# Second MLP: Strassen products accumulated on one another in open PSUM tiles instead of being added up in SBUF

## Chip, cores and metric

The kernel runs on one core of a Trainium2 chip. The metric is the device time of one execution in microseconds (us); of several executions the median counts.

## What is computed

Attention through packed keys, a squared-ReLU MLP, and a second MLP with a softmax and a layer norm between its two products. The change lies in the last function.

```python
def _moe_ref(x, w_in, w_out):                      # 4608 tokens, 512 -> 2048 -> 512
    h = np.maximum(x @ w_in, 0.0)
    return h * h @ w_out

def _moe2_ref(x, w_in, w_out, g_ln):               # 4608 tokens, 512 -> 1024 -> 512
    h = x @ w_in
    e = np.exp(h - np.max(h, axis=-1, keepdims=True))
    solu = h * (e / (np.sum(e, axis=-1, keepdims=True) + 1e-09))
    mu = np.mean(solu, axis=-1, keepdims=True)
    var = np.mean((solu - mu) ** 2, axis=-1, keepdims=True)
    return ((solu - mu) / np.sqrt(var + 1e-06) * g_ln) @ w_out
```

## The kernel before

Attention and the first MLP fill the execution up to about 800 us; their matmuls are those of line 58. The second MLP then goes over the 4608 tokens in 18 pairs of 128-token halves (256 tokens each). The loop at the end of `build` runs, for step `i`, `h2(i+1)` (first product, softmax, layer norm), `fetch_y` (loads the operands of a later pair), `ou(i-1)` (second product and output) and `tr(i)` (transposes of the normed rows and the operands of `ou`). `h2(0)` and the start of pair 1 lie inside the last steps of the first MLP.

Both products of a pair are done as 2 by 2 blocks by `strassen`, with seven block products instead of eight. `prod(l, r)` makes one block product: for each of `nk` chunks of 128 rows three matmuls (high part by high part, high by low, low by high, since every operand is split into two parts), all added up in one PSUM tile. In `h2` it has `nk` = 2 and 512 columns, so six matmuls a product, into tiles named `h`; in `ou` `nk` = 4 and 256 columns, twelve matmuls, into tiles `o`. The seven products are 11 by 11, 12 by 21, S2 by T2, S3 by T3, S1 by T1, S4 by 22 and 22 by T4; with the weights `wi0T2` (first chunk, operand T2) and `wx0` to `wx6` (11, T1, 22, 21, T3, T2, T4 of the first chunk) a row of TensorE tells which product it belongs to.

Before the change every product has a PSUM tile of its own. The first is copied out twice by ScalarE (lines 842 and 843). Three `add`s (`vadd`, line 854) bring products into the blocks `c12` and `c21` in SBUF on VectorE, and four `fin`s bring the rest; in `h2` `fin` is line 865, which also keeps the row maximum, in `ou` it is line 854 as well. So a row `hs L854` is an `add` of `h2`, a row `ys L854` an `add` or a `fin` of `ou`:

```python
        p1 = prod("11", "11")
        A.copy(c11, p1)
        A.copy(c12, p1)
        fin(0, c11, c11, prod("12", "21"))
        add(c12, c12, prod("S2", "T2"))
        add(c21, c12, prod("S3", "T3"))
        p5 = prod("S1", "T1")
        add(c12, c12, p5)
        fin(1, c22, c21, p5)
        fin(0, c12, c12, prod("S4", "22"))
        fin(1, c21, c21, prod("22", "T4"))
```

The tiles `h` and the tiles `o` have three PSUM banks each in the loop (`psh`, `pso`), with one more bank each for the transposes `ct`; pair 0 uses four banks that it shares with the first MLP. A product can begin when the product three before it in the same pool has been read.

In this part no order is written out. A scheduler sets it for each engine from its own estimates of durations, and an engine then does its instructions in that order: one that waits holds up all behind it on that engine. Other names: `ch`/`cl` are the high and low parts of `ou`'s operands (lines 1037 and 1038), `raw` the transposed blocks and their sums (lines 1053 and 1043), `e` the exponential (878), `hs` the rows of `h2` (`hs L891` and `hs L895` apply the layer norm), `rstd` a power on GpSimd (889).

## Time and profile before

| what | us |
|---|---|
| three executions | 1203.02, 1203.15, 1207.12 (median 1203.15) |
| profiled execution, first to last instruction (span) | 1198.6 |
| its TensorE busy | 1144.2 (95%) |
| its VectorE, ScalarE, GpSimd busy | 878.9, 665.0, 568.6 |
| TensorE's granted clock over the span | 0.990 |

The time of an execution is the span and some microseconds around it; the profiled execution's own time isn't among the three, so the difference between the median and the span, 4.55 us, is taken for what lies around. Instructions are counted busy from start to end. A matmul is pipelined: its end is modelled, and the next one starts before that end. So the spacing of the starts tells how fast TensorE works, and a row that TensorE "sat idle" before is a true wait.

### The profile page before, as it was taken

The page shows a single profiled execution, that of the slowest core. Times are in us where ns is not written, and L with a number is a line of the kernel's source. Part 1 is how long each engine was busy: PE and PEld are TensorE (multiplying, and loading weights), DVE is VectorE, ACT ScalarE, POOL GpSimd, SP SyncE. Part 2 cuts the span into 40 slices and gives each one's busy share as a digit, 9 for nine tenths or more (in the row PEclk, how much of TensorE's full clock was granted, in tenths as well). Part 3 has the DMA queues.
Part 4 walks back from the last instruction along what each step waited for, and adds up shares of the span by engine and source line. Part 5 has one row for each costly group of instructions (what it writes and reads, how often), then busy time and mean ns, then how long its engine had stood idle before and what let it go on. Part 6 is the DMA issues. An engine that isn't in the chain of part 4 may idle for free. (4 is left out here: it accounts for less than half of the span.)

```text
span 1198.6 us, 24126 instructions
## 1 busy us (share of the span) xinstructions
PE 1144.2 (95%) x8700; PEld 1049.8 (88%) x8700; DVE 878.9 (73%) x1705; ACT 665.0 (55%) x1510; POOL 568.6 (47%) x585
## 2 busy tenths in 40 slices
PE   6788999999999999999999999999999999999997
PEld 3466989898999998999998999988888899899897
DVE  4787688755326766567888977258989889889887
ACT  3575665344445555566675776435554655655554
POOL 0002354534225544475776775213754755745743
PEclk9889999999999999999999999999999999999999
DMA  9767697665155799779598796991133133223201
GB/s 326 229 185 204 181 300 234 211 210 197 57 200 151 207 302 298 215 276 334 203 384 316 257 379 245 387 342 74 61 133 102 41 132 106 84 84 111 80 23 49
DMA packets 124343, 236.99 MB, mean 198 GB/s; under 512 B 16576, under 2 KB 44224, under 8 KB 124224
## 3 DMA queue, kind: packets, MB, share of 16 engines
q1 hardware_dynamic: 124224, 235.46, 58.7%
q8 instruction: 68, 1.11, 0.4%
q14 instruction: 51, 0.42, 0.1%
HBM read 144.18 MB, written 91.23 MB: 196 GB/s over the span
## 5 line engine op out<-in xcount | busy, mean ns | idle before, releaser
L58 PE MATMUL Y<-ghl,woh 128*128 128x288 f32 x2048 | 463.9, 302 | 6.1 <-DVE yp L493 3.4
L58 PEld LDWEIGHTS Y<-ghl,woh 128*128 128x128 f32 x2048 | 345.4, 190 | 20.6 <-issue 6.1
L58 PE MATMUL Y<-ghl,wol 128*128 128x288 f32 x1024 | 304.2, 297 | 0.0
L58 PE MATMUL h<-ah,slot 128*128 128x288 f32 x1024 | 212.9, 296 | 10.3 <-ACT ah L432 9.0
L837 PE MATMUL o<-wx,ch 128*128 128x256 f32 x1008 | 190.2, 286 | 5.3 <-DVE ys L854 3.0
L58 PEld LDWEIGHTS Y<-ghl,wol 128*128 128x128 f32 x1024 | 194.6, 190 | 0.0
L1038 POOL TENSOR_TENSOR cl<-raw,ch 128x512 fp32r<-128x512 f32 x100 | 148.3, 1502 | 92.4 <-ACT ch L1037 47.0
L58 PEld LDWEIGHTS h<-ah,slot 128*128 128x128 f32 x1024 | 165.0, 189 | 12.6 <-ACT ah L432 9.5
L469 POOL TENSOR_TENSOR rg<-rg 128x288 f32<-128x288 f32 x128 | 92.8, 726 | 166.5 <-ACT rg L462 151.7
L837 PEld LDWEIGHTS o<-wx,ch 128*128 128x128 f32 x1008 | 158.9, 190 | 12.3 <-DVE ys L854 4.5
L58 PE MATMUL h<-al,slot 128*128 128x288 f32 x512 | 150.9, 295 | 1.0 <-DVE al L67 1.0
L837 PE MATMUL o<-wx,cl 128*128 128x256 f32 x504 | 142.1, 285 | 2.2 <-POOL cl L1038 1.7
L67 DVE TENSOR_TENSOR ghl<-rg,ghl 128x288 fp32r<-128x288 f32 x149 | 79.2, 537 | 80.2 <-POOL rg L469 63.2
L462 ACT ACTIVATE rg<-h 128x288 f32<-128x288 f32 x148 | 60.3, 408 | 98.0 <-PE h L58 95.0
L1037 ACT CAST ch<-raw 128x512 fp32r<-128x512 f32 x126 | 76.7, 622 | 61.0 <-DVE raw L1043 57.6
L53 DVE TENSOR_TENSOR ghl<-rg,ghl 128x288 fp32r<-128x288 f32 x107 | 78.2, 743 | 29.2 <-ACT ghl L53 15.6
L837 PEld LDWEIGHTS o<-wx,cl 128*128 128x128 f32 x504 | 95.4, 190 | 4.4 <-POOL cl L1038 2.5
L58 PEld LDWEIGHTS h<-al,slot 128*128 128x128 f32 x512 | 96.2, 188 | 1.6 <-DVE al L67 1.6
L53 ACT ACTIVATE rg<-h 128x288 f32<-128x288 f32 x108 | 44.3, 410 | 84.7 <-PE h L58 81.0
L837 PE MATMUL h<-wi,y 128*128 128x512 f32 x312 | 83.6, 402 | 0.3 <-DVE hs L854 0.3
L1043 DVE TENSOR_TENSOR raw<-raw 128x512 f32<-128x512 f32 x70 | 73.6, 1060 | 9.9 <-POOL cl L1038 5.0
L470 ACT ACTIVATE ghl<-rg 128x288 fp32r<-128x288 f32 x148 | 65.8, 445 | 20.6 <-PE Y L58 17.5
(172 smaller groups left out, 2097.7 us busy)
## 6 DMA issues: line engine op xcount, KB each, us to landing
pw_d<-pws SPq DMA_DIRECT2D x122, 256.0 KB, 4.5
slot<-pw_d SPq DMA_DIRECT2D x61, 512.0 KB, 6.0
yc_d<-yo SPq DMA_DIRECT2D x98, 256.0 KB, 5.6
y<-yc_d SPq DMA_DIRECT2D x92, 256.0 KB, 4.3
raw<-w_in SPq DMA_DIRECT2D x40, 512.0 KB, 6.5
raw<-w_out SPq DMA_DIRECT2D x24, 512.0 KB, 6.0
kf<-kT SPq DMA_DIRECT2D x32, 288.0 KB, 6.1
out<-ys SPq DMA_DIRECT2D x72, 128.0 KB, 1.7
```

Source lines behind the costliest of these rows:

```text
L53: return (lambda *a, **k: pin(fn(*a, **k))) if strict[0] else fn
L58: pin(PE.matmul(*a, **k))
L67: eng.tensor_tensor(out=lo, in0=x, in1=f(hi), op=ALU.subtract)
L462: A.activation(r, pb[:, :HF], AF.Relu)
L469: G.tensor_tensor(out=gg, in0=r, in1=r, op=ALU.mult)
L470: A.activation(gh, r, AF.Square)
L837: PE.matmul(bk, x, w[:, y], start=(i == 0), stop=(i == 3 * nk - 1))
L1037: A.copy(c[n][0], x)
L1038: eng.tensor_tensor(out=c[n][1], in0=x, in1=f(c[n][0]), op=ALU.subtract)
L1043: eng.tensor_tensor(out=out, in0=x, in1=y, op=op)
```

## The change

Products that share a sum are now accumulated on one another in one PSUM tile that stays open. `prod` takes a tile `bk` to go on with. Tile `u` takes 11 by 11, then S2 by T2, then S3 by T3; ScalarE copies it out after each of the three, into `c11`, `c12` and `c21`. Tile `p5` takes S1 by T1, is read by the `fin` of `c22`, and then takes S4 by 22. The three `add`s are gone and the four `fin`s stay; one copy by ScalarE is added, since there are three and not two. TensorE's matmuls are the same in number and kind. Between two products on one tile TensorE has to wait until the tile has been read; a Strassen now has four tiles and not seven.

```diff
-    def strassen(lhs, rhs, nk, N, pb, c11, c12, c21, c22, add, fin):
-        def prod(l, r):
-            bk = pb()[:, :N]
+    def strassen(lhs, rhs, nk, N, pb, c11, c12, c21, c22, fin):
+        def prod(l, r, bk=None):
+            new = bk is None
+            if new:
+                bk = pb()[:, :N]
             i = 0
             for k in range(nk):
                 lh, ll = lhs(l, k)
                 w = rhs[k][r]
                 for x, y in ((lh, 0), (lh, 1), (ll, 0)):
-                    PE.matmul(bk, x, w[:, y], start=(i == 0), stop=(i == 3 * nk - 1))
+                    PE.matmul(bk, x, w[:, y], start=(new and i == 0), stop=(i == 3 * nk - 1), skip_group_check=not new)
                     i += 1
             return bk
 
-        p1 = prod("11", "11")
-        A.copy(c11, p1)
-        A.copy(c12, p1)
+        u = prod("11", "11")
+        A.copy(c11, u)
         fin(0, c11, c11, prod("12", "21"))
-        add(c12, c12, prod("S2", "T2"))
-        add(c21, c12, prod("S3", "T3"))
+        prod("S2", "T2", u)
+        A.copy(c12, u)
         p5 = prod("S1", "T1")
-        add(c12, c12, p5)
+        prod("S3", "T3", u)
+        A.copy(c21, u)
         fin(1, c22, c21, p5)
-        fin(0, c12, c12, prod("S4", "22"))
         fin(1, c21, c21, prod("22", "T4"))
+        prod("S4", "22", p5)
+        fin(0, c12, c12, p5)
```

The two callers no longer hand `vadd` over. In the changed file the lines behind `strassen` stand three lower: 842/843 become 844, 847 and 850 (the copies of `u`), 854 becomes 857, 1037 becomes 1040.

The scheduler makes a new order of the second MLP. Three places show it. The first is the Strassen of pair 0 on TensorE, inside the first MLP; of the two chunks of a product the first stands here.

Before:

```order
L837 MATMUL h_10111<-wi011_9780,y0_9742 128x512 x3
...
L837 MATMUL h_10120<-wi021_9814,y0_9743 128x512 x3
...
L837 MATMUL h_10129<-wi0T2_9846,y0_9744 128x512 x3
...
L837 MATMUL h_10137<-wi0T3_9878,y0_9745 128x512 x3
...
L837 MATMUL h_10145<-wi0T1_9913,y0S1_9746 128x512 x3
...
L837 MATMUL h_10155<-wi022_9960,y0S4_9747 128x512 x3
...
L837 MATMUL h_10164<-wi0T4_9992,y022_9748 128x512 x3
...
L58 MATMUL Y0_618<-ghl_10015,woh9_2004 128x288
```

After, on the same engine at the same place:

```order
L839 MATMUL h_10111<-wi011_9780,y0_9742 128x512 x3
...
L839 MATMUL h_10119<-wi021_9814,y0_9743 128x512 x3
...
L839 MATMUL h_10135<-wi0T1_9913,y0S1_9746 128x512 x3
...
L839 MATMUL h_10111<-wi0T2_9846,y0_9744 128x512 x3
...
L839 MATMUL h_10111<-wi0T3_9878,y0_9745 128x512 x3
...
L839 MATMUL h_10135<-wi022_9960,y0S4_9747 128x512 x3
L839 MATMUL h_10135<-wi122_9962,y0S4_9747 128x512 x3
L58 MATMUL Y0_618<-ghl_10015,woh9_2004 128x288
...
L839 MATMUL h_10151<-wi0T4_9992,y022_9748 128x512 x3
```

S3 by T3 now comes directly behind S2 by T2 on the same tile `h_10111`, S4 by 22 directly behind S3 by T3, and 22 by T4 has gone behind twelve matmuls of the first MLP.

The second place is the Strassen of `ou` for pair 14, in the middle of the run, on TensorE; the first row of each product stands here. Before:

```order
L837 MATMUL o_14607<-wx0_9842,ch_14432 128x256 x2
...
L837 MATMUL o_14622<-wx3_9876,ch_14434 128x256 x2
...
L837 MATMUL o_14636<-wx5_9911,ch_14436 128x256 x2
...
L837 MATMUL o_14650<-wx4_9909,ch_14438 128x256 x2
...
L837 MATMUL o_14664<-wx1_9844,ch_14440 128x256 x2
...
L837 MATMUL o_14679<-wx2_9874,ch_14442 128x256 x2
...
L837 MATMUL o_14693<-wx6_9942,ch_14444 128x256 x2
```

After, for the same pair, with the product of `h2` (`h_14368`) and the transposes that stand between:

```order
L839 MATMUL o_14452<-wx0_9842,ch_14282 128x256 x2
...
L839 MATMUL o_14466<-wx3_9876,ch_14284 128x256 x2
...
L1036 MATMUL ct_14565<-ident_68,hs_14060 128x128 x3
L839 MATMUL o_14493<-wx1_9844,ch_14290 128x256 x2
...
L839 MATMUL o_14452<-wx5_9911,ch_14286 128x256 x2
...
L839 MATMUL h_14368<-wi022_9960,y2_14158 128x512 x3
...
L839 MATMUL o_14520<-wx6_9942,ch_14294 128x256 x2
...
L839 MATMUL o_14452<-wx4_9909,ch_14288 128x256 x2
...
L839 MATMUL o_14493<-wx2_9874,ch_14292 128x256 x2
```

Between two products on one tile the scheduler has put other products: 12 by 21 and S1 by T1 ahead of S2 by T2, 22 by T4 ahead of S3 by T3. On ScalarE the three copies of the same tile stand so, after the change:

```order
L1040 CAST ch_14292<-raw_14308 128x512
L850 COPY hs_14343<-h_14344 128x512
L844 COPY ys_14451<-o_14452 128x256
L847 COPY ys_14451<-o_14452 128x256
L1056 COPY raw_14570<-ct_14565 128x512
L881 ACTIVATE e_14403,sm3_14404<-hs_14342,nm2_14401 128x1024
L1040 CAST ch_14551<-raw_14570 128x512
...
L881 ACTIVATE e_14422,sm3_14423<-hs_14343,nm2_14420 128x1024
L850 COPY ys_14451<-o_14452 128x256
```

The first two copies follow each other, so ScalarE stands from the one to the end of S2 by T2; the third comes behind an exponential that waits for VectorE.

The third place is the last Strassen, that of `ou` for pair 17, at the end of TensorE's queue. Before:

```order
L837 MATMUL o_15200<-wx0_9842,ch_15141 128x256 x2
...
L837 MATMUL o_15229<-wx5_9911,ch_15145 128x256 x2
...
L837 MATMUL o_15257<-wx1_9844,ch_15149 128x256 x2
...
L837 MATMUL o_15243<-wx11_10022,ch_15147 128x256 x2
...
L837 MATMUL o_15272<-wx2_9874,ch_15151 128x256 x2
...
L837 MATMUL o_15286<-wx6_9942,ch_15153 128x256 x2
```

After:

```order
L1036 MATMUL ct_15000<-ident_68,hs_14612 128x128
L839 MATMUL o_15025<-wx0_9842,ch_14966 128x256 x2
...
L839 MATMUL o_14908<-wx2_9874,ch_14816 128x256 x2
...
L839 MATMUL o_15066<-wx1_9844,ch_14974 128x256 x2
...
L839 MATMUL o_15093<-wx6_9942,ch_14978 128x256 x2
...
L839 MATMUL o_15025<-wx4_9909,ch_14972 128x256 x2
...
L839 MATMUL o_15066<-wx2_9874,ch_14976 128x256 x2
```

The last product is now S4 by 22 on `o_15066`, directly behind S3 by T3; the `fin` that reads `o_15066` before it needs the copy of S3 by T3's tile.

## Rows read from the trace of the kernel before

**Rows 1.** The page's first line.

```profile
span 1198.6 us, 24126 instructions
```

**Rows 2.** Busy time by stretch: stretch, its length, PE, PEld, DVE, ACT, POOL, clock, DMA share, GB/s.

```profile
840.00:885.00 45.00, 41.69 (x278) 37.14 (x277) 43.36 (x88) 24.97 (x45) 30.62 (x26) 1.00 0.23 77
885.00:1160.00 275.00, 271.77 (x1763) 245.28 (x1762) 241.70 (x513) 156.75 (x279) 159.93 (x128) 1.00 0.28 91
1160.00:1198.60 38.60, 32.36 (x267) 31.46 (x265) 29.32 (x59) 17.10 (x31) 12.98 (x10) 1.00 0.13 42
```

**Rows 3.** PE's waits, 760 to 1199 us: us in total, times, longest.

```profile
PE o L837 <- DVE ys L854: 3.0, 3, 1.8
PE o L837 <- POOL cl L1038: 1.7, 2, 1.4
...
PE o L837 <- ACT ys L843: 1.2, 1, 1.2
```

**Rows 4.** Groups by line, 885 to 1160 us: count, busy us, mean ns, idle before.

```profile
L854 DVE TENSOR_TENSOR ys<-ys,o 128x256 f32<-128x256 f32 x85 | 33.7, 409 | 0.6 <-PE o L837 0.3
...
L854 DVE TENSOR_TENSOR hs<-hs,h 128x512 f32<-128x512 f32 x39 | 26.5, 679 | 1.5 <-PE h L837 0.5
...
L1038 DVE TENSOR_TENSOR cl<-raw,ch 128x512 fp32r<-128x512 f32 x12 | 10.8, 898 | 2.6 <-ACT ch L1037 2.6
...
L842 ACT COPY hs<-h 128x512 f32<-128x512 f32 x13 | 7.6, 586 | 0.0
...
L842 ACT COPY ys<-o 128x256 f32<-128x256 f32 x13 | 4.8, 368 | 0.0
```

**Rows 5.** Timeline (start, length, engine), one stop of PE and what ended it.

```profile
1140.78 0.40 PE L837 MATMUL o<-wx,ch 128*128 128x256 f32 x2
1141.02 0.28 PE L837 MATMUL o<-wx,cl 128*128 128x256 f32 x1
1141.89 0.50 PE L837 MATMUL o<-wx,ch 128*128 128x256 f32 x2 [0.60 <-DVE ys L854]
1142.24 0.28 PE L837 MATMUL o<-wx,cl 128*128 128x256 f32 x1
...
1141.42 0.42 DVE L854 TENSOR_TENSOR ys<-ys,o 128x256 f32<-128x256 f32 x1
```

**Rows 6.** Timeline of pair 0's Strassen: PE, then the first ACT copy and DVE `fin`.

```profile
778.70 2.98 PE L837 MATMUL h<-wi,y 128*128 128x512 f32 x12
781.52 0.86 PE L837 MATMUL h<-wi0T,y 128*128 128x512 f32 x3
...
787.51 0.93 PE L837 MATMUL h<-wi0T,y 128*128 128x512 f32 x3 [0.28 <-DMA wi0T<-wi_d]
788.68 0.96 PE L837 MATMUL h<-wi1T,y 128*128 128x512 f32 x3 [0.24 <-DMA wi1T<-wi_d]
...
780.31 0.58 ACT L842 COPY hs<-h 128x512 f32<-128x512 f32 x1 [0.46 <-PE h L837]
...
781.82 0.69 DVE L865 CUSTOM_DVE_ANT_0 hs<-hs,h 128x512 f32<-128x512 f32 x1 [1.21 <-PE h L837]
```

**Rows 7.** Timeline of the end: `h2`'s last matmuls, PE's last stops, DVE's last addition.

```profile
1159.38 0.86 PE L837 MATMUL h<-wi1T,y 128*128 128x512 f32 x3
...
1174.33 0.50 PE L837 MATMUL o<-wx,ch 128*128 128x256 f32 x2 [0.84 <-ACT ch L1037]
1176.39 1.07 PE L1033 MATMUL ct<-ident,hs 128*128 128x128 f32 x8 [1.55 <-DVE hs L891]
1177.98 0.39 PE L837 MATMUL o<-wx,cl 128*128 128x256 f32 x1 [0.52 <-DVE cl L1038]
...
1195.31 0.42 DVE L854 TENSOR_TENSOR ys<-ys,o 128x256 f32<-128x256 f32 x1 [1.01 <-PE o L837]
```

**Rows 8.** ACT's waits, 885 to 1160 us: us in total, times, longest.

```profile
ACT ch L1037 <- DVE raw L1043: 41.3, 30, 4.5
ACT hs L895 <- DVE nb L894: 17.8, 13, 2.9
```

## Prediction of the time after the change

> **What bounds the kernel now.** I read the busy time by stretch first. From 885 to 1160 us, thirteen of the eighteen pairs, TensorE is busy 271.77 of 275 us at the full granted clock, VectorE 241.70, ScalarE 156.75 [rows 2]. The change takes work from VectorE and leaves TensorE's matmuls as they are, so it can win only where TensorE stops; the second view is therefore TensorE's waits [rows 3]. VectorE's additions lead them with 3.0 us, and the 1.2 us for ScalarE's copy are theirs in part, since ScalarE's queue waits on VectorE too [rows 8]. All idle time of TensorE is 3.31 us from 840 to 885, 3.23 us from 885 to 1160, and 2.91 us in three stops near the end [rows 2, 7]. Pair 0 adds 0.28 and 0.24 us for weights [rows 6].
>
> A stop costs more than its idle row. In the timeline of one, two 256-column matmuls start 0.24 us apart, 0.12 each. The next ought to start at 1141.14 and starts at 1141.89; the one behind it comes 0.35 us later where 0.24 is usual [rows 5]. That is 0.75 + 0.11 = 0.86 us for a row of 0.60, so 0.26 us on top. With three, five and three stops the stretches hold 3.31 + 0.78 = 4.1, 3.23 + 1.3 = 4.5 and 2.91 + 0.78 = 3.7 us; pair 0 holds 0.52 + 0.52 = 1.0. Together 13.3 us, 1.1% of the time: no more is to be had.
>
> **The change, part by part.**
>
> *VectorE's additions.* Three of 679 ns and three of 409 ns go in every pair [rows 4], 3.26 us in some 21 us; at 88% busy [rows 2] that is about a sixth of its work. ScalarE gets one copy of 0.59 and one of 0.37 us more [rows 4], and was busy 57% of the stretch. Neither is worth anything in itself, since TensorE bounds both; worth lies in the stops. From 840 to 885, where VectorE is busy 43.36 of 45 us [rows 2], all three stops come from its lateness (1.8 us for an addition, 1.2 for a copy queued behind a cast that waited for it, and a small one). I take back three quarters: **-3.0** (bounds 0 and -4.1). From 885 to 1160 two stops for `ys` weigh 1.2 us idle (3.0 less the one of 1.8), two for GpSimd's `cl` 1.7 [rows 3], and the fifth, for an addition of `h2`, what is left of 3.23, 0.3. The additions' 1.5 us and 3 x 0.26 I take as gone, 2.3; `cl` is work that the change leaves alone, but in the new order S1 by T1, whose operand is ready earlier than S2's, is the third product, so of 1.7 + 0.52 I take half, 1.1: **-3.4** (bounds 0 and -4.5). What is late next is whatever else feeds TensorE: GpSimd's splits and ScalarE's casts.
>
> *The new waits in pair 0.* In the order, S3 by T3 follows S2 by T2 directly on one tile, and S4 by 22 follows S3 by T3 while `fin` still has to read its tile. Price of the first: the first product's six matmuls take 6 x 0.235 us (twelve take from 778.70 to 781.52), so it ends its turn at 780.11; the copy begins at 780.31 and takes 0.58 [rows 6]; TensorE resumes 0.05 us after a releaser ends [rows 5]. 0.20 + 0.58 + 0.05 + 0.11 of restart = 0.94 us. The second has a copy and a `fin` in a row: 0.20 + 0.58 + about 0.03 + 0.69 [rows 6] + 0.05 + 0.11 = 1.66. Nothing else stands on TensorE there, so nothing hides them: 2.6 us. ScalarE is free there and queues no more than the exponential behind the copies. Pair 1 has one product (1.4 us) between S3 by T3 and S4 by 22 where 1.55 are needed: 0.3. **+2.9** (bounds 2.5 and 4). On the other side 22 by T4 now comes after twelve matmuls of the first MLP, so its weights have landed: **-1.0**.
>
> *The new waits in the middle.* In pairs 2 to 16 I counted in the order what stands between two products on one tile. The shortest stretch in `ou` is 24 matmuls of 0.12 us, 2.9 us, and mostly 3.2 to 5; in `h2` it is 3.7. Needed are 0.20 + 0.37 + 0.05 = 0.62 and 0.83 us. So the copy hides, with at least 2.2 us to spare, as long as ScalarE comes to it in time. ScalarE does its queue in order, and ahead of the copies stand casts and exponentials that wait for VectorE; before, such casts waited 41.3 us in 30 waits, 1.4 each, 4.5 at the longest [rows 8]. Behind a copy that waits for TensorE stand the copies of `ct` to `raw`, on which VectorE and GpSimd wait; the order puts them where their transposes come later anyway. The trace of before has no such pair of products, so I bound it: 0 if every wait stays below 2.2, 7.7 if eight of sixteen pairs meet one of 2.9 (2.9 - 2.2 + 0.26 = 0.96 each). The mean of 1.4 is nearer to the lower end: **+1.5**.
>
> The Trainium skill speaks against this part: in "Perfetto Trace Analysis", section Matmuls, it asks that independent groups of matmuls rotate through PSUM banks, so that one is copied out while the next runs. By that rule each of the three stops of a chain would be paid in full; how much that is stands under the rivals. The order agrees with it in pair 0 and at the end, where the products do follow each other.
>
> *The end.* Before, the last matmul of `h2` ends at 1159.38 + 0.86 = 1160.24, and the last transposes start at 1176.39, after softmax and norm: 16.15 us [rows 7], with VectorE busy nearly all of it. In the new order VectorE has on that way four `ys` additions fewer and two `cl` splits more, -4 x 0.41 + 2 x 0.90 = +0.2 us [rows 4]; TensorE has 24 matmuls more and 7 transposes fewer to do meanwhile, some 2.0 us. So the two stops of 0.84 and 1.55 shrink to one of about 0.55. The last product is S4 by 22 behind S3 by T3: 0.20 + 0.37 + 0.03 + 0.42 + 0.05 + 0.11 = 1.2 us that nothing covers. With the stop of 0.52 for `cl`, 0.55 + 0.52 + 0.52 + 1.2 = 2.8 instead of 3.7: **-0.9** (bounds -2 and +1.5). Behind the last matmul stand, as before, one addition (1195.31) and the output's transfer.
>
> **Sum.** -3.0 - 3.4 + 2.9 - 1.0 + 1.5 - 0.9 = -3.9 us on the span of 1198.6 [rows 1]: 1194.7. The median of the runs, 1203.15, lies 4.55 us above the span, so 1199.3 us, 0.3% less. About 0.5%, 6 us, is what a measurement of this kernel can tell from no change.
>
> **The rivals.**
>
> *All old stops go and no new ones come in the middle.* -4.1 - 4.5 + 2.9 - 1.0 + 0 - 0.9 = -7.6, so 1195.6. For it: nearly all stops trace back to VectorE, which sheds a sixth of its work. Against it: GpSimd's two stops, and that the first pairs fill a pipeline in which something is late anyhow.
>
> *VectorE's relief buys nothing.* The scheduler's estimates stay what they were; if its order runs ScalarE's casts or GpSimd as late as VectorE ran, the old stops come back under other names. Then -1.0 + 2.9 = +1.9: 1205.1. For it: only 3.0 of TensorE's waits name an addition.
>
> *ScalarE comes late to the copies, slower than before.* A copy of `u` stands behind an exponential or cast that waits for VectorE, and TensorE stands behind the copy. If one wait of 2.9 us, as `hs` has it [rows 8], lies ahead of a copy in every one of sixteen pairs, it costs 16 x 0.96 = 15.4 us; with half of the relief (-3.2), +2.9, -1.0 and -0.9 that is +13.2, 1216.4. It ends above the old time from 2.2 / 16 = 0.14 us a pair, and above 0.5% from 0.5 us a pair. For it: the third copy of pair 14 stands behind an exponential. Against it: waits above 2.2 us were few, and a VectorE with a sixth less to do is late less often.
>
> *No overlap at all*, the skill's rule as a mechanism of this kernel: every copy stops TensorE. In `h2` 2 x 0.94 + 1.66, in `ou` 2 x 0.73 + 1.2, together 6.2 us a pair, 112 us in eighteen: 1315. The order has other products between in sixteen pairs, so this needs the order not to do what it says.
>
> **How the numbers follow.** Chances: the forecast 0.45 (1196.5 to 1203), all stops gone 0.22 (1194 to 1197), relief worth nothing 0.16 (1203 to 1207), ScalarE late 0.15, no overlap 0.02. The limits of 0.5% are 1197.1 and 1209.2. Faster: the second case and 0.05 of the first, 0.27. Slower: ScalarE late and no overlap, 0.17. The same: 0.56. The range from 1194 to 1207.5 holds the first three cases, 0.8 of the chance.
>
> **What would show it.** Right, if the stops for `ys` additions are gone from TensorE's waits, VectorE's share from 885 to 1160 falls to some 73%, TensorE waits about 0.8 us for a copy and 1.4 for a `fin` in pair 0, and about 1 us for a `fin` ahead of the last product. Wrong, if TensorE's waits name the copies (lines 844, 847, 850) in the middle, if its idle time there is not below 3.2 us, or if the last transposes wait for `hs` longer than before.

## The result, and the profile after

The changed kernel takes 1210.63 us (median of 6 executions, 1208.8 to 1212.01), the kernel before 1203.09 us (6, 1200.41 to 1207.12): 1.0057 times as long, 95% interval 1.0041 to 1.0073. That is slower by 0.6%, and above the predicted range (1194.0 to 1207.5). Executions of one kernel spread by some us with TensorE's granted clock: of 126 later ones of the kernel before, the 54 with a clock of 0.989 or more over the span have a median of 1201.8 us, the other 72 one of 1205.0; the changed kernel's six have clocks from 0.987 to 0.989.

The page's first line and the busy time by stretch (columns as in [rows 2], which these answer):

```profile
span 1208.4 us, 23964 instructions
```

```profile
840.00:885.00 45.00, 43.01 (x282) 38.74 (x282) 36.52 (x77) 29.58 (x57) 28.41 (x25) 1.00 0.24 77
885.00:1160.00 275.00, 269.65 (x1758) 243.53 (x1757) 216.25 (x443) 166.50 (x303) 147.75 (x127) 1.00 0.28 91
1160.00:1208.40 48.40, 41.13 (x303) 38.78 (x302) 32.30 (x60) 23.04 (x42) 17.32 (x13) 0.96 0.11 36
```

VectorE's busy time from 885 to 1160 us fell from 241.70 to 216.25 us (79% of the stretch, where 73% was predicted), and TensorE's fell as well, from 271.77 to 269.65: an engine with a tenth less to do, and TensorE stops more, not less (5.35 us idle, where the prediction called itself wrong from 3.2 on). TensorE's waits from 760 us on (us in total, times, longest), which answer [rows 3]:

```profile
PE o L839 <- DVE ys L857: 7.2, 6, 1.7
PE h L839 <- DVE mx L868: 2.1, 3, 1.4
PE ct L1036 <- ACT hs L898: 1.7, 2, 0.9
PE o L839 <- POOL cl L1041: 1.2, 1, 1.2
PE o L839 <- DVE cl L1041: 0.8, 1, 0.8
PE h L839 <- ACT hs L847: 0.7, 1, 0.7
PE h L839 <- ACT hs L850: 0.7, 1, 0.7
```

The additions' waits are gone, since there are no additions. In their place stand waits for `fin`s (`ys L857`, and `mx L868` in `h2`), and two of the transposes for the layer norm (`hs L898`).

To compare kernels I add up, over the whole timeline from the first `h2` matmul of pair 0 to TensorE's last matmul, by how much two successive matmuls start farther apart than the median of their kind. This holds the idle time, the slow start behind a stop, and lost clock. TensorE's work is the same in all kernels, so these sums must explain the difference, and they do: that distance is 416.29 us before and 423.48 after, 7.19 more, and the sums are 14.6 and 21.8.

| us lost by TensorE | pairs 0 and 1 (first 60 us) | 60 to 106 us (before: up to 885) | on to `h2`'s last matmul | the end | sum |
|---|---|---|---|---|---|
| before | 1.1 | 5.0 | 5.0 | 3.6 | 14.6 |
| changed | 4.3 | 2.7 | 7.8 | 7.1 | 21.8 |
| predicted change | +1.9 | -3.0 | -1.9 | -0.9 | -3.9 |
| measured change | +3.2 | -2.3 | +2.8 | +3.5 | +7.2 |

Ahead of pair 0 the program is the same, and executions differ by some us there by themselves (the first `h2` matmul starts at 778.70 in the profiled execution before, at 781.30 after).

**Pair 0.** TensorE's timeline (start, length) shows the two new waits:

```profile
787.74 0.97 PE L839 MATMUL h<-wi0T,y 128*128 128x512 f32 x3 [0.68 <-ACT hs L847]
...
790.82 1.43 PE L839 MATMUL h<-wi,y0S 128*128 128x512 f32 x5 [1.40 <-DVE mx L868]
```

With restarts they cost 0.83 and 1.57 us, where 0.94 and 1.66 were predicted; the waits for weights [rows 6] are gone, as predicted. **Pairs 1 and 2** were not foreseen so:

```profile
817.22 0.97 PE L839 MATMUL h<-wi,y 128*128 128x512 f32 x3 [0.68 <-ACT hs L850]
...
834.58 0.97 PE L839 MATMUL h<-wi,y 128*128 128x512 f32 x3 [0.50 <-DVE mx L868]
```

At 817.22 us TensorE waits for ScalarE's third copy. In the order the waiting product is 11 by 11 of pair 2, directly behind S3 by T3 of pair 1:

```order
L839 MATMUL h_10377<-wi0T3_9878,y1S3_9949 128x512 x3
...
L839 MATMUL h_10532<-wi011_9780,y2_10352 128x512 x3
```

It opens a new tile and needs a bank. Of the three, `p5` of pair 1 still holds one and 22 by T4 has another, so it takes that of `u`, which is free only when `u` has been copied out for the third time. I had priced the waits between two products on one tile, and not the next pair's wait for the bank that an open tile holds. With the restart it costs 0.83 us; the 0.3 us that I had ahead of S4 by 22 of pair 1 did not come, since this same product stands between. The stop at 834.58, 0.66 us with the restart, is of the kind that I had counted: S4 by 22 of pair 2 waits for the `fin` that reads its own tile. I had put that wait at nothing in pair 2; VectorE came to the `fin` only at 833.84, behind two `raw`.

**The middle.** It has four stops of over 1 us. Here is the first of them, PE's row first and then VectorE, ScalarE and GpSimd ahead of it:

```profile
922.45 0.50 PE L839 MATMUL o<-wx,ch 128*128 128x256 f32 x2 [1.66 <-DVE ys L857]
...
916.22 3.49 DVE L1046 TENSOR_TENSOR raw<-raw 128x512 f32<-128x512 f32 x2
919.63 1.25 DVE L897 SCALAR_TENSOR_TENSOR nb<-mv,rstd 128x1 f32<-128x1 f32 x1
920.80 1.27 DVE L887 BATCH_NORM_STATS2 st<-hs 128x6 f32<-128x512 f32 x2
922.00 0.39 DVE L857 TENSOR_TENSOR ys<-ys,o 128x256 f32<-128x256 f32 x1
...
918.09 0.62 ACT L1040 CAST ch<-raw 128x512 fp32r<-128x512 f32 x1 [2.11 <-DVE raw L1046]
...
915.49 6.60 POOL L1041 TENSOR_TENSOR cl<-raw,ch 128x512 fp32r<-128x512 f32 x4
```

The waiting product is S1 by T1 of a new pair. By the order it stands 4.9 us of TensorE's work behind S4 by 22 of the pair before, and of the three `o` banks the new `u` and the new 12 by 21 have two, so it needs the third, that of the old `p5`. VectorE had 4.9 us to read `p5`, but did two `raw`, a `nb` and two `st` first (`st` are the statistics for the norm), from 916.22 to 922.00: the `raw` took 1.74 us each and `nb`, the norm's bias, a column of 128x1, 1.25, beside GpSimd's `cl`. Five of the six waits for `ys` are of this kind, the first product on a new `p5` behind the late last `fin` of the old one; the sixth is the wait ahead of the last product (1.07 us; 1.2 predicted). Another such stop of 1.8 us comes at 1099.26, with the same instructions in the same order ahead of it, and two of 1.0 us for the layer norm at 967.12 and 1143.79.

**The end.** Two stops, with restarts 1.13 us for a `fin` and 1.38 for GpSimd's `cl`, and then the granted clock falls; behind it come two more, 0.95 us for a `cl` and the 1.07 ahead of the last product:

```profile
1180.66 0.50 PE L839 MATMUL o<-wx,ch 128*128 128x256 f32 x2 [0.97 <-DVE ys L857]
1182.39 0.39 PE L839 MATMUL o<-wx,cl 128*128 128x256 f32 x1 [1.23 <-POOL cl L1041]
...
1203.36 0.51 PE L839 MATMUL o<-wx,ch 128*128 128x256 f32 x2 [0.92 <-DVE ys L857]
```

Busy time by stretch:

```profile
1176.60:1182.60 6.00, 3.80 (x29) 3.40 (x29) 6.00 (x10) 2.64 (x6) 5.19 (x4) 1.00 0.20 67
1182.60:1186.60 4.00, 4.00 (x22) 4.00 (x22) 3.34 (x9) 1.67 (x3) 2.06 (x2) 0.57 0.12 39
```

From 1182.6 to 1186.6 us the granted clock is 0.57, mostly the lower level (1.2 of 2.4 GHz): 22 matmuls where a stretch as long in e6 (below) holds 36.

### The profile page after: what moved, and what is told of

The parts are those of the page before. It is cut to its first block, busy times and chain, and to the rows that moved or that the text cites. A ratio compares the mean times of both kernels' runs of the same rounds, so it can differ in the third digit from the quotient of the medians.

```text
span 1208.4 us, 23964 instructions
## 1 busy us (share of the span) xinstructions
PE 1146.8 (95%) x8700; PEld 1052.6 (87%) x8700; DVE 840.0 (70%) x1597; ACT 680.5 (56%) x1546; POOL 557.1 (46%) x585
```

## The experiments

Theories, as they came up: **A**, open tiles of `ou` hold its banks; **B**, it is the order that the scheduler made anew, and any edit moves the stops about; **C**, only the new waits of pair 0 and of the end count; **D**, the open tiles stretch `h2`, which then comes too late at the end; **F**, the end is limited by the last `ou` and VectorE; **G**, VectorE's relief went into waits for GpSimd; **H**, in `h2` it is `p5` that costs. For mixed kernels `strassen` has both forms:

```diff
+    def strassen(lhs, rhs, nk, N, pb, c11, c12, c21, c22, fin, add=None):
...
+        if add is not None:
+            p1 = prod("11", "11")
...
+            return
         u = prod("11", "11")
```

(between stands the form before the change, with seven tiles and three `add`s).

All results, with the lost time by stretch as in the table above (sums are of the profiled execution, medians and intervals of all):

| run | us, median | ratio to before, 95% interval | pairs 0, 1 | to 106 us | middle | end | sum |
|---|---|---|---|---|---|---|---|
| e1 `h2` alone | 1214.67 | 1.0079 to 1.0123 | 5.7 | 2.1 | 9.2 | 10.5 | 27.4 |
| e2 `ou` alone | 1196.22 | 0.9924 to 0.9956 | 1.1 | 2.8 | 3.0 | 3.9 | 10.7 |
| e3 `u` alone | 1204.39 | 0.9994 to 1.0021 | 4.0 | 4.1 | 2.5 | 5.6 | 16.2 |
| e4 `p5` alone | 1207.97 | 1.0026 to 1.0055 | 1.8 | 3.2 | 10.8 | 3.5 | 19.2 |
| e5 last `h2` old | 1212.69 | 1.0046 to 1.0096 | 4.3 | 2.7 | 7.6 | 10.6 | 25.1 |
| e6 pair 0 old | 1206.26 | 1.0000 to 1.0035 | 2.8 | 2.4 | 7.8 | 5.6 | 18.6 |
| e7 `ou` but the last | 1199.28 | 0.9951 to 0.9986 | 1.1 | 2.7 | 2.1 | 5.6 | 11.5 |
| e8 order of lines alone | 1204.13 | 0.9988 to 1.0027 | 2.7 | 5.0 | 6.7 | 3.4 | 17.8 |
| e9 short `nb` | 1203.63 | 0.9970 to 1.0009 | 4.2 | 2.3 | 3.1 | 6.6 | 16.1 |
| e10 `ou`, and `u` of `h2` | 1206.14 | 1.0004 to 1.0036 | 4.4 | 5.0 | 3.2 | 5.6 | 18.3 |
| e11 `ou`, short `nb` | 1198.00 | 0.9931 to 0.9973 | 2.0 | 0.8 | 4.5 | 2.7 | 10.0 |
| e12 `ou`, and `p5` of `h2` | 1202.79 | 0.9967 to 1.0004 | 2.2 | 3.5 | 4.6 | 5.5 | 15.9 |
| e13 long `nb`, order of e9 | 1204.82 | 0.9992 to 1.0024 | 4.2 | 2.5 | 4.2 | 6.6 | 17.5 |
| e14 short `nb`, order of e9 | 1204.25 | 0.9985 to 1.0019 | 4.1 | 2.0 | 2.7 | 5.9 | 14.7 |
| e15 before, short `nb` | 1197.23 | 0.9916 to 0.9966 | 1.2 | 1.6 | 3.5 | 4.0 | 10.3 |
| e16 pairs 0, 1 old, short `nb` | 1196.77 | 0.9929 to 0.9967 | 1.6 | 0.1 | 2.8 | 6.5 | 11.0 |
| e17 another order | 1201.78 | 0.9959 to 1.0002 | 4.8 | 1.6 | 1.0 | 6.0 | 13.3 |
| e18 `h2` alone, short `nb` | 1212.81 | 1.0051 to 1.0108 | 7.2 | 1.6 | 5.7 | 10.9 | 25.4 |

### Which half, which tile (e1 to e4)

```diff
-                 ob[0][0], ob[0][1], ob[1][0], ob[1][1], fin)
+                 ob[0][0], ob[0][1], ob[1][0], ob[1][1], fin, vadd)
```

This is e1; e2 has the same edit in `h2`'s call instead.

> The open tiles in h2 alone (products of 512 columns, pair 0 among them); ou adds up in SBUF as before. Reference points: 1203.1 us before, 1210.6 after. Theory A (open tiles of ou hold two of its three banks, so that a product stands until a late addition of VectorE has freed its bank): the loss lies in ou, so this keeps only pair 0's 1.6 us net and gains from 39 hs additions gone; about 1202 to 1205, and no stop above 1.2 us for a ys addition behind 885 us beyond the two of before. Theory B (the scheduler's new order as such: any change of the code moves some stops about): anywhere from 1200 to 1210, and the changes of the two halves do not add up to 7.5 us. Theory C (VectorE's relief is worth nothing, and only the new waits of pair 0 and of the end count): 1203.1 + 1.6 = 1204.7, the stretch from 885 to 1160 us as before (3.2 us idle).

> The open tiles in ou alone (products of 256 columns); h2 adds up in SBUF as before, also in pair 0. Theory A (banks of ou held by open tiles): the ys waits of TensorE, 7.2 us in six stops in the changed kernel, come back here, against 3.0 in three before; 1207 to 1210. Theory B (order as such): anywhere from 1200 to 1210. Theory C (only pair 0 and the end): 1203.1 plus the end's 3.9 us, 1207.0, with 3.2 us idle from 885 to 1160 us.

It came out the other way round. With open tiles in `ou` alone the kernel is 7.7 us faster than before, with open tiles in `h2` alone 10.7 us slower. Theory A, as a loss that lies in `ou`, fell. TensorE's waits of e2 (its `strassen` stands lower, so 857 is 830 here), and of e1:

```profile
PE o L842 <- DVE ys L830: 3.0, 4, 0.9
PE ct L1050 <- ACT raw L1070: 1.0, 1, 1.0
```

```profile
PE o L842 <- ACT ch L1054: 8.3, 6, 2.9
PE h L842 <- DVE mx L882: 3.7, 3, 1.9
PE o L842 <- DVE cl L1055: 2.4, 1, 2.4
```

In e1 TensorE waits for `ou`'s operands (`ch`, `cl`), which are made from `h2`'s result through norm and transposes.

For e3 and e4 one of the chains is taken apart, in both halves, first `p5` (e3), then `u` (e4):

```diff
         p5 = prod("S1", "T1")
+        vadd(c12, c12, p5)
...
-        prod("S4", "22", p5)
-        fin(0, c12, c12, p5)
+        fin(0, c12, c12, prod("S4", "22"))
```

```diff
-        u = prod("11", "11")
-        A.copy(c11, u)
+        p1 = prod("11", "11")
+        A.copy(c11, p1)
+        A.copy(c12, p1)
...
-        prod("S2", "T2", u)
-        A.copy(c12, u)
+        vadd(c12, c12, prod("S2", "T2"))
...
-        prod("S3", "T3", u)
-        A.copy(c21, u)
+        vadd(c21, c12, prod("S3", "T3"))
```

> In both halves only tile u stays open (11 by 11, S2 by T2, S3 by T3); S4 by 22 has a tile of its own, and one addition on VectorE (c12 plus S1 by T1) is back, so five tiles in a Strassen and one bank held throughout instead of two. Theory A: a fin of p5 no longer holds a bank until the end of the Strassen, so of the 7.5 us about half is gone: 1205 to 1208, with ys waits of TensorE around 3 to 5 us. Pair 0 keeps its copy's wait of 0.9 us but not the 1.6 us before S4 by 22. The end has no wait for a fin ahead of the last product (1.1 us less). Theory B: anywhere from 1200 to 1210. Theory C: pair 0 and the end are worth 2.7 us less than in the changed kernel, 1207.9.

> In both halves only tile p5 stays open (S1 by T1, then S4 by 22); 11 by 11, S2 by T2 and S3 by T3 have tiles of their own and two additions on VectorE are back, so six tiles in a Strassen. Theory A: one bank held from S1 by T1 to the last fin; the loss of 7.5 us falls by about half: 1205 to 1208. Theory B: anywhere from 1200 to 1210. Theory C: of the new waits pair 0 has one (a fin only, 0.2 + 0.7 + 0.2 = 1.1 us less the product ahead of it), the end keeps its 1.1 us: 1206 to 1208. If VectorE's load counts, this and the kernel with u alone lie between the two: VectorE's share from 885 to 1160 us about 84% here, 81% there, 79% with all chains and 88% before.

E4 lies between before and changed; e3 can't be told from before. In e4 the middle loses 10.8 us, nearly all of it in one kind of wait, S4 by 22 of `h2` for the `fin` that still reads its tile (eight of these nine waits; the first is pair 0's):

```profile
PE h L842 <- DVE mx L867: 9.0, 9, 1.5
```

That is the wait that the change adds, paid, with 0.3 to 1.7 us a time, where the scheduler puts S4 by 22 too early. In e3 the middle loses 2.5. Set against before, the medians of the two halves add up to +3.0 us and those of the two chains to +4.4, where the change costs 7.5. Either the parts work on one another or the new order of each kernel does it; these runs don't separate the two.

### The end and pair 0 (e5, e6), the last Strassen (e7), the order of lines (e8)

```diff
-                 t[0][:, 0], t[0][:, 1], t[1][:, 0], t[1][:, 1], fin)
+                 t[0][:, 0], t[0][:, 1], t[1][:, 0], t[1][:, 1], fin, vadd if m >= NPAIR - 1 else None)
```

This is e5; e6 has `m == 0` as the condition.

> The changed kernel, but h2 of the last pair (17) adds up in SBUF as before. In the order nothing moves ahead of that pair, and behind the last matmul of h2 there are 31.2 us of TensorE's work instead of 27.9 (31.3 before). In all six kernels measured so far 33.8 to 36.5 us pass from the last h2 matmul to the last matmul of all, whatever work is left for it (25.8 to 31.6 us). Theory D (the open tiles stretch h2's Strassen; the last h2 comes out later, and the chain softmax, norm, transposes, products behind it stays as long with less work to cover it): about 3.3 us less than the changed kernel, and 1 to 2 more if the granted clock no longer falls near 1181 us; 1205 to 1207.5. Theory B (any change of the order moves the stops about): no reason for a gain here; 1210.6 within 2 us. Theory F (the end is limited by the last ou's own chain and by VectorE, not by when the last h2 comes): 1210 to 1212, with the last h2 earlier and the same end.

> The changed kernel, but h2 of pair 0 adds up in SBUF as before; the order behind pair 1 is that of the changed kernel. The stops of 0.83 and 1.57 us for the copy and the fin of pair 0 go, the waits for the weights of T2 or T4 come back (0.52 idle, 1.0 with restarts): 2.4 + 0.2 - 1.0, so 1.2 to 1.6 us less than the changed kernel, 1209.2. If the time goes into the waits behind it instead (pair 1's 0.83 and 0.66, VectorE's and ScalarE's queues behind the first pairs), 1210.6.

In e5 the stops ahead of the last pair come back to a hundredth (1.82 us at the same place, 1.03, 0.34, 1.82, 1.04): the same order gives the same stops in another execution. The last `h2` did come earlier, 384.80 us behind the first instead of 388.26, and the end took 42.0 us instead of 35.2, with new stops of 3.2, 1.7 and 1.5 us and a fall of the clock. So Theory D's constant end fell: what is behind the last `h2` depends on the order as well. F came near in the time, but its end that stays the same did not show either: this one is 6.8 us longer, and the kernel is not faster.

E6 gains 4.4 us in the medians, more than the 1.2 to 1.6 expected, and 3.2 us in the sums: 1.5 in pairs 0 and 1, as expected, and 1.5 at the end, because the clock did not fall in the profiled execution. Its end has the same stops (1.15 and 1.38 us for 1.13 and 1.38), and the stretches that answer to those of the changed kernel read

```profile
1175.20:1181.20 6.00, 3.79 (x29) 3.38 (x29) 6.00 (x8) 2.41 (x4) 5.74 (x4) 1.00 0.15 49
1181.20:1185.20 4.00, 4.00 (x36) 4.00 (x35) 2.25 (x6) 2.17 (x5) 0.55 (x1) 1.00 0.07 19
```

E7 is e2 with the last Strassen of `ou` as before:

```diff
-                 ob[0][0], ob[0][1], ob[1][0], ob[1][1], fin)
+                 ob[0][0], ob[0][1], ob[1][0], ob[1][1], fin, vadd if m >= NPAIR - 1 else None)
```

> Open tiles in ou of pairs 0 to 16 only; h2 everywhere and ou of the last pair as before the change. Differs from the kernel with open tiles in all of ou (1196.2) in the last Strassen alone, where the last product waited 0.95 us for a fin. Theory D: that wait goes and the rest stays, 1.0 us less: 1195.2. Theory B: anything from 1194 to 1204. If the addition that is back on VectorE at the very end stands in the output's way instead, 1196 to 1197.

The wait of 1.08 us ahead of the last product is gone; one for `cl` grew from 0.95 to 2.43 us in its place, and the end is no shorter (5.6 us instead of 3.9): the 1.0 us less that Theory D had did not come. E8 is the kernel before with two of its lines moved:

```diff
-        add(c21, c12, prod("S3", "T3"))
         p5 = prod("S1", "T1")
+        add(c21, c12, prod("S3", "T3"))
         add(c12, c12, p5)
         fin(1, c22, c21, p5)
-        fin(0, c12, c12, prod("S4", "22"))
         fin(1, c21, c21, prod("22", "T4"))
+        fin(0, c12, c12, prod("S4", "22"))
```

> The kernel before with the products written in the new order (S1 by T1 third, 22 by T4 sixth, S4 by 22 last), but each in a tile of its own and with the three additions: nothing is accumulated across products. Matmuls, copies and additions are those of before, so only the scheduler's order differs. Theory B (order luck): it may lie as far from 1203.9 as the other kernels do, 5 us or more to either side. Theory D: h2 of the last pair spans 15.2 us of TensorE's work (12.9 before, 19.2 in the changed kernel) and 30.5 us are left behind it instead of 31.3: 0.8 us more at the end, so 1204 to 1206.

No difference in time that the runs can tell, though the stops lie elsewhere. Theory B allowed 5 us or more to either side; this order did not move the time.

### VectorE and GpSimd (e9 to e14)

In the changed kernel VectorE shed 35 of the 85 `ys` additions of [rows 4] and all 39 of `hs` from 885 to 1160 us, 35 x 0.409 + 39 x 0.679 = 40.8 us, and its busy time fell by only 25.4. Three groups that answer to [rows 4]:

```profile
L1046 DVE TENSOR_TENSOR raw<-raw 128x512 f32<-128x512 f32 x49 | 52.5, 1084 | 2.7 <-POOL cl L1041 2.4 <-ACT raw L1056 0.3
...
L1041 DVE TENSOR_TENSOR cl<-raw,ch 128x512 fp32r<-128x512 f32 x13 | 16.8, 1291 | 4.0 <-ACT ch L1040 3.9
L897 DVE SCALAR_TENSOR_TENSOR nb<-mv,rstd 128x1 f32<-128x1 f32 x19 | 16.0, 841 | 2.7 <-POOL rstd L892 2.7
```

`cl` has 1291 ns instead of 898, `nb` 841 instead of 321 (6.1 us in 19 before). These two grew by 6.0 and 9.9 us, 15.9 in all; `raw`, the costliest, did not grow (56.5 us in 52 before). Set against GpSimd's rows, the 15 `nb` that overlap one take 1023 ns, the other four 156; `raw` 1119 and 684, `cl` 1472 and 684. A `fin`, which reads PSUM, takes 0.4 us either way. The Trainium skill, "SBUF — State Buffer", section "Who interferes with whom", says that an instruction of VectorE with two inputs from SBUF contends with one of GpSimd that reads SBUF, and one with at most one such input doesn't, outside VectorE's two-port modes; the rows of `nb`, `raw`, `cl` and `fin` agree. The condition matters here: the norm's `hs L894`, with one such input of 128x1024, takes 812 ns alone and 1774 beside GpSimd's `cl`, so it is not so that all instructions with one input take the same, as the expectation below has it. So `nb` in a form with one input:

```diff
-                V.scalar_tensor_tensor(out=nb, in0=mv[:, 0:1], scalar=-1.0, in1=rstd, op0=ALU.mult, op1=ALU.mult)
+                V.tensor_scalar(out=nb, in0=rstd, scalar1=mv[:, 0:1], scalar2=-1.0, op0=ALU.mult, op1=ALU.mult)
```

> The changed kernel with one small instruction of VectorE in another form: nb (the norm's bias, 128x1) by a tensor_scalar with one input from SBUF and the mean as its scalar, instead of a scalar_tensor_tensor with two inputs from SBUF. In the changed kernel nb took 156 ns where GpSimd was idle and 1023 ns in the 15 of 19 times where GpSimd was running, as the subtractions of two SBUF inputs do (684 and 1119 ns), while VectorE's instructions that read PSUM or one input take the same with and without. Theory G (VectorE's relief was lost to waits for GpSimd, and its late fins and late nb make the four stops of 1.82, 1.82, 1.04 and 1.04 us in the middle): nb at about 150 ns throughout, each of the four stops shorter by about 1.1 us or gone, all stops from the first h2 matmul on 18 us instead of 22; 1206 to 1207.5. Theory B (the order as such): nb shorter as well, but the stops as large in other places, 20 to 24 us in all; 1209 to 1212.

7 us less than the changed kernel, below both forecasts, and the middle lost 3.1 instead of 7.8: it looked like Theory G. But the edit changes the scheduler's estimate too, and the order with it. Beside it other mixtures were run: e2 with one chain of `h2` added (e10 the `u` of e3, e12 the `p5` of e4, in the branch `if add is not None` that `h2` takes), and e2 with the short `nb` (e11).

```diff
+        if add is not None:
+            u = prod("11", "11")
...
+            fin(0, c12, c12, prod("S4", "22"))
+            return
```

> Open tiles u and p5 in ou, and in h2 tile u alone (its S4 by 22 in a tile of its own, one addition back). Between the kernel with open tiles in ou alone (1196.2, stops of 10.9 us from the first h2 matmul on) and the changed kernel (22.1 us). Theory H (in h2 it is tile p5 that costs: S4 by 22 waits for a fin that stands late in VectorE's queue, as the 9.0 us of mx waits with p5 alone): here only pair 0 and pair 1 pay 0.83 us each for a copy and the middle stays near 2 to 3 us; 1198 to 1200. Theory D (each chain stretches h2, 17.7 us of TensorE's work against 14.6): 27.9 us are left behind the last h2 matmul instead of 31.6, and the middle pays as well; 1201 to 1205.

> Open tiles in ou alone, with nb in the form of one input. In the kernel with open tiles in ou alone nb met GpSimd only 2 times in 18, so Theory G gives little: 0 to 1.5 us less than that kernel, 1195 to 1196.5. Theory B: the order moves once more, 1194 to 1202.

> Open tiles u and p5 in ou, and in h2 tile p5 alone (11 by 11, S2 by T2 and S3 by T3 in tiles of their own, two additions back). Theory H (tile p5 of h2 is what costs): pair 0 pays 1.6 us, and mx waits come back in the middle, 5 to 9 us in all; 1203 to 1207. Theory D (any chain in h2 stretches it): 30.0 us are left behind the last h2 matmul, 1.6 less than with ou alone; 1199 to 1203.

H fell: added to `ou`, tile `u` of `h2` costs 9.9 us and `p5` 6.6 (1206.14 and 1202.79 less 1196.22), more than the predicted 2 to 4 for `u`, and `u` more than `p5`. E11 is within 2 us of e2, on the slower side.

To tell G from B, `nb` got a form with two inputs that the scheduler prices as e9's, so that all engines have e9's order:

```diff
+                V.scalar_tensor_tensor(out=nb, in0=rstd, scalar=mv[:, 0:1], in1=mone, op0=ALU.mult, op1=ALU.mult)
```

This is e13; e14 has e9's line, and the constant `mone` of -1 as well, which it doesn't use.

> The changed kernel in the order of the kernel with nb of one input, on every engine, but nb again as a scalar_tensor_tensor with two inputs from SBUF (rstd and a constant -1, the mean as scalar). Theory G (two inputs from SBUF make nb wait for GpSimd, and that makes the stops): nb at 0.9 to 1.0 us wherever GpSimd runs (14 of 20 times), and stops in the middle of 5 to 8 us instead of 3.0; 3 to 5 us more than e14. Theory B (the order is what helped): nb long as well, but the stops as in e14 to 1 us.

> The partner of e13: the changed kernel with nb of one input (206 ns), with the same order. Under both theories the stops of the kernel measured before in this form: 3.9 us in pairs 0 and 1, 2.1 up to 885 us, 3.0 in the middle, 4.5 at the end (and 2 more where the granted clock falls); 1203.6 within 2 us.

```profile
L899 DVE SCALAR_TENSOR_TENSOR nb<-rstd,mv,mone 128x1 f32<-128x1 f32 x20 | 17.1, 854 | 2.4 <-POOL rstd L894 2.3
```

```profile
L899 DVE TENSOR_SCALAR nb<-rstd,mv 128x1 f32<-128x1 f32 x19 | 3.9, 207 | 2.8 <-POOL rstd L894 2.7
```

In one order `nb` takes 13.2 us more in e13 than in e14, and VectorE is busy 7.0 us more from 885 to 1160 us (216.23 and 209.18). That is worth 1.5 us in the middle, less than Theory G had (2 to 5) and more than Theory B (1). Of the 2.8 us in all sums 1.7 are a fall of the clock at 1177 us that only e13's profiled execution has; the medians lie 0.6 us apart, which the runs can't tell from nothing. So of e9's 4.7 us in the middle some 1.5 were `nb` at most, and the rest the order. Only `nb` was tested so: what the two `raw` beside `cl` cost (1.74 us each at the first stop, 0.68 alone) has no such pair of runs.

### The order itself (e15 to e18)

E15 is the kernel before with e9's line for `nb`.

> The kernel before the change with nb of one input. There nb met GpSimd 6 times in 19, 0.53 us each, 3.2 us of VectorE's time in the middle, and no stop of TensorE named the norm. Theory G: 0 to 1.5 us less than before, 1202 to 1204. Theory B: the order moves, 1199 to 1208. If nb's form is worth as much here as in the changed kernel (7 us), it has nothing to do with the change: 1196 to 1197.

The kernel before gains 6 us by the same edit of `nb`, close to the third forecast, though only 6 of its 19 `nb` met GpSimd. By that forecast the gain has nothing to do with the change. It keeps all additions, with VectorE busy 243.72 us from 885 to 1160:

```profile
885.00:1160.00 275.00, 272.90 (x1778) 246.79 (x1778) 243.72 (x520) 157.10 (x279) 159.14 (x129) 1.00 0.28 91
```

E16 has e9's line too, and

```diff
-                 t[0][:, 0], t[0][:, 1], t[1][:, 0], t[1][:, 1], fin)
+                 t[0][:, 0], t[0][:, 1], t[1][:, 0], t[1][:, 1], fin, vadd if m < 2 else None)
```

> The changed kernel with nb of one input and with h2 of pairs 0 and 1 as before the change. Of the 3.9 us of stops in pairs 0 and 1 some 0.9 for weights remain: 3 us less than e14, 1200.5. Theory D (the open tiles of h2 also cost behind pair 1, whatever nb's form): 1200 to 1201 at best, still above the 1196.2 with open tiles in ou alone. Theory G alone (nothing else is wrong with the open tiles of h2): as good as that, 1196 to 1198.

It comes to 1196.8: with pairs 0 and 1 left alone the change is neither better nor worse than e15, which doesn't have it. E14, which has it in pairs 0 and 1 as well, takes 7.0 us more than e15. The control is e17, the changed kernel with two of its lines moved:

```diff
         A.copy(c11, u)
-        fin(0, c11, c11, prod("12", "21"))
+        p5 = prod("S1", "T1")
         prod("S2", "T2", u)
         A.copy(c12, u)
-        p5 = prod("S1", "T1")
+        fin(0, c11, c11, prod("12", "21"))
```

> The changed kernel with the first lines of its Strassen in another order (S1 by T1 second, the fin of 12 by 21 after the copy of S2 by T2): the same tiles, matmuls, copies, fins and waits, nb as in the changed kernel with two inputs. Theory B (the middle and the end are a matter of the order): stops of pairs 0 and 1 as in the changed kernel (3.9 us), those of the middle and of the end anything from 5 to 14 us; 1202 to 1210, and not where the changed kernel lies. Theory D (the open tiles of h2 cost in every order): 1209 to 1212, with middle and end at 13 us or more.

1201.78 us, 8.9 less than the changed kernel, with the same tiles, matmuls, copies, `fin`s and two-input `nb`: Theory D fell for the changed kernel, and Theory B's 1202 to 1210 held but for 0.2 us. Its middle and its waits:

```profile
885.00:1160.00 275.00, 274.75 (x1805) 250.16 (x1804) 215.27 (x452) 168.37 (x306) 158.03 (x131) 1.00 0.28 91
```

```profile
PE h L839 <- DVE mx L868: 2.4, 2, 1.4
PE o L839 <- DVE ys L857: 2.4, 3, 1.1
PE o L839 <- ACT ch L1040: 1.8, 2, 1.1
```

VectorE is as busy as in the changed kernel (215.27 and 216.25), ScalarE too, and TensorE stands still for 0.25 us instead of 5.35. The `raw` meet GpSimd as often (48 of 52, 1137 ns each, for 45 of 49 and 1119), so their length alone makes no stops. Pairs 0 and 1 keep their price (the same 0.83, 1.57 and 0.83 us), and the end keeps 6.0.

E18 is e1 with e9's line for `nb`.

> Open tiles in h2 alone, with nb of one input, which makes another order. With nb of two inputs it took 1214.7 us, with stops of 5.3 us in pairs 0 and 1, 7 in the middle and 7 at the end, and 5 in stretches where the granted clock fell. Theory B: pairs 0 and 1 stay at 4 to 5 us, the rest falls to the level of the other kernels; 1202 to 1207. Theory D (the open tiles of h2 are bad where ou has seven tiles): 1211 to 1215.

Open tiles in `h2` alone stay bad in a second order, 1212.81 us. So there it isn't one unlucky order. In this order TensorE does wait for a copy in the middle, three times, 0.83, 0.76 and 0.80 us (S3 by T3 of `h2` for the copy of line 864, that of S2 by T2): the wait that the prediction named. Why `ou`'s operands come late when `h2` has open tiles and `ou` has seven tiles was not settled.

The one edit of `nb` moved four kernels by -6.1 us (before), -7.0 (changed), +1.8 (`ou` alone) and -1.9 (`h2` alone). A shorter `nb` can't explain such a spread; the new order that comes with the edit can.

## Why the prediction was wrong, step by step

**What bounds it**: right. The time follows TensorE's stops: in the changed kernel and the eighteen runs the median less the sum of the table lies between 1185.5 and 1189.6 us, though the sums go from 10.0 to 27.4.

**VectorE's additions.** The old stops went, up to 885 us 2.3 of the predicted 3.0 us, and in the middle those for `ys` additions and most of those for `cl`. That the relief took them away isn't shown: e15 keeps every addition and loses 1.6 us up to 106 and 3.5 in the middle, where before lost 5.0 and 5.0. The step that failed is the sentence behind it, "What is late next is whatever else feeds TensorE", to which I gave no price: by the terms the middle should have lost 5.0 - 3.4 + 1.5 = 3.1 us, and it lost 7.8. VectorE's load was taken for the cause of its lateness. It isn't: with VectorE busy 243.72 of 275 us the middle lost 3.5 us (e15), with 216.25 it lost 7.8 (changed), and with 215.27 it lost 1.0 (e17). In the stops read, what counts is what stands ahead of a `fin` in VectorE's queue, and the scheduler sets that anew with every edit. The load didn't fall as predicted either: 15.9 us of the 40.8 came back in a longer `nb` and `cl`.

**The new waits in pair 0**: right in kind and size (0.83 and 1.57 us; the weights' waits gone). The pairs behind it were mis-sized, 1.5 us instead of 0.3: 0.83 because a tile that stays open also keeps its bank from the next pair, 0.66 because the `fin` ahead of pair 2's S4 by 22 came late. All the kernels with open `u` and `p5` in `h2` of pair 0 lose 4.1 to 7.2 us in pairs 0 and 1, against 1.1 before.

**The new waits in the middle.** Estimated at 1.5 us within 0 to 7.7; four new stops took 1.82 + 1.04 + 1.83 + 1.03 = 5.7. They are not those that I had named: from 888 to 1160 us no wait names a copy of lines 844, 847 or 850. Two are for the last `fin` of `p5`, on which the next pair's `p5` waits, and two for the norm. I counted the work between two products on one tile, and left out the work between the last read of a tile and the next tile in its bank. In the order of e17 6.8 us of the middle's 7.8 are not there, and in that of e9 4.7 are not: they belong to the one order that the scheduler happened to make.

**The end.** -0.9 predicted within -2 to +1.5, +3.5 measured. The wait ahead of the last product was right (1.07 for 1.2). The stop of the last transposes is gone (0.55 were left to it), but two others came: 1.13 us for a `fin` behind a multiplication by `e` that took 2.32 us on VectorE instead of 1.28, and 1.38 for GpSimd's own `cl`. Some 2 us went with the clock; a fall of it was in no term, and whether it falls is luck as far as these runs show (last section). The rest is not the order alone: in three orders of the changed kernel (its own, that of e9, e13 and e14, and e17) the end loses 5.9 to 7.1 us, in three of the kernel before (its own, e8, e15) 3.4 to 4.0. Beyond the wait of 1.07 us, why stayed open.

**The rivals.** "Relief buys nothing" (1205.1, 0.16) described it best, down to "the old stops come back under other names". E13 and e14 came out there (1204.8 and 1204.3), by luck in part: against before e14 loses 5.3 us less from 60 us on to the last `h2` matmul, and 5.3 more in pairs 0 and 1 and at the end. The changed kernel lies above by its order. "ScalarE late" didn't happen in the changed kernel. "No overlap" didn't either: 4.9 us of work stand between the products at the worst stop of the middle. The rule of the Trainium skill behind it ("Perfetto Trace Analysis", Matmuls) holds where the order puts nothing between, with 0.83, 1.57 and 1.07 us a time, and in part in e4's nine waits (0.3 to 1.7 us). No rival said that the order itself may be worth as much as 9 us, as between the changed kernel and e17, and the range should have had that.

**The span and the median.** I added 4.55 us for what lies around the span. In the 126 later executions of the kernel before it is 1.73 to 1.86, so the profiled execution of before took about 1200.4, and was one of the shorter of its kind. The forecast starts from the median, so this does not move it.

## What to carry to other kernels

Where a scheduler writes the order anew, first measure what a new order does without a change: here the same arithmetic took 1210.6 and 1201.8 us, and an edit of a 128x1 instruction moved the kernel before by 6 us, nearly as much as the change cost. So no single pair of kernels says what such a change is worth. Open tiles in `ou` alone took 1196.2 and 1198.0 us in two orders, and the kernel before took 1203.8 (the median of all 126 executions), 1204.1 and 1197.2 in three: a gain from open tiles isn't shown. A tile that stays open saves additions, but holds its bank until its last reader, so price the next user of the bank and not only the next product on the tile. In three orders of the changed kernel pairs 0 and 1 lose 4.1 to 4.8 us, in three of the kernel before 1.1 to 2.7. Take load off an engine only after finding that its load, and not the place of one instruction in its queue, makes the others wait.

## What the runs showed of the hardware

A `nb` of 128x1 took 156 ns alone and up to 1250 ns beside GpSimd's `cl`; with one input from SBUF it took 207 beside GpSimd and 206 without. The granted clock fell to 0.57 for 4 us in the changed kernel behind 6 us in which TensorE was busy 3.80, and did not fall in e6 behind 6 us with 3.79 busy and the same two stops. Behind longer stops (3.2 us in e5, 3.0 in e1) it fell as well, in e5 to

```profile
1176.40:1182.00 5.60, 5.60 (x27) 5.60 (x28) 3.28 (x7) 3.18 (x6) 0.55 (x1) 0.50 0.21 70
```

The stops alone do not decide it. E9 and e14 have the same order on every engine and, in the first stretch shown, the same three stops (0.49, 1.34 and 0.54 us in e9, 0.49, 1.35 and 0.54 in e14); the clock fell in e9 and not in e14:

```profile
1169.80:1175.80 6.00, 4.11 (x30) 3.49 (x29) 5.53 (x10) 2.15 (x4) 4.92 (x4) 1.00 0.18 63
1175.80:1179.20 3.40, 3.40 (x18) 3.40 (x17) 3.40 (x6) 2.27 (x3) 1.32 (x1) 0.50 0.03 10
```

```profile
1174.66:1180.66 6.00, 4.10 (x30) 3.49 (x29) 5.52 (x10) 2.15 (x4) 4.92 (x4) 1.00 0.18 62
1180.66:1184.06 3.40, 3.24 (x27) 3.04 (x27) 3.40 (x6) 2.27 (x3) 1.33 (x1) 1.00 0.06 16
```

So one profiled execution doesn't tell whether a kernel pays for a fall. What decides it no run shows.
